# Dropping semaphore waits between the two banks of one PSUM tile, in an attention and token-mixing kernel

## The chip, the cores and the metric

The kernel runs on one core of one Trainium2 chip. The metric is the device time of one execution in microseconds (us), as a median over several executions. The profile's span is a little shorter than the timed run, because it leaves out what stands before the first and after the last instruction. Engines are named as in the profile: PE (matrix products), PEld (its weight loads), DVE (vector), ACT (scalar), POOL (gpsimd), SP (the engine that issues all DMAs here). PSUM is the memory into which PE writes its products, in eight banks; copying a finished product out of it is called an evacuation. A semaphore wait holds an engine until another engine's instruction is marked as done.

## The reference

Eight batches of 576 positions, eight heads of 64. A sliding-window attention with a distance bias is followed by a layer that mixes tokens:

```python
def _attn_ref(q, k, v):
    scores = scale * np.matmul(q, k.transpose(0, 1, 3, 2))
    mask = (rel >= 0) & (rel < window)                 # window = 128
    scores = np.where(mask, scores + bias[None], -1000000000.0)
    ...                                                # softmax
    return np.matmul(attn, v)

def _moe_ref(x, w_q, w_k, w_out):
    wq = x @ w_q
    wk = x @ w_k
    W_tok = scale * np.einsum('bsd,btd->bst', wq, wk)
    mixed = np.einsum('bst,btd->bsd', W_tok, x)
    return np.maximum(mixed, 0.0) @ w_out
```

The kernel writes the second layer as G = wk^T x, then relu(wq G), then the product with `w_out`.

## The kernel before

The work is a fixed list of 765 steps. Each step has an engine and, where it writes or reads PSUM, a bank; `PLAN` holds all of that as text, so no scheduler decides anything. Eight banks are held as four tiles of two banks each, because several steps (scores and their exponentials, transposes of q and k, MX and its relu) use two banks as one tensor. Other steps (products with `w_k` and `w_q`, G, the transposes of x, the output blocks) use one bank of a pair.

```python
pairs = [pp.tile([P, 1024], FP32, name=f"bank{i}") for i in range(4)]

def bank(b):
    return pairs[b // 2][:, 512 * (b % 2) : 512 * (b % 2) + 512]
...
def f_out(eng, bk, b=b, t=t):          # one output block: PE fills one bank
    for db in range(4):
        nc.tensor.matmul(bank(bk[0]), rm[:, b % 2, db, P * t : P * t + P],
                         wout_sb[:, db, :], start=(db == 0), stop=(db == 3))

def f_oute(eng, bk, t=t, n=n):         # ACT or DVE empties it
    copy(eng, osb[n % 3][:, t % 2, :], bank(bk[0]))
...
if t % 2:
    def f_store(eng, bk, b=b, t=t, n=n):   # two blocks leave in one DMA
        nc.sync.dma_start(out=out[b, P * (t - 1) : P * (t + 1), :].rearrange(...), in_=osb[n % 3])
...
def f_storet(eng, bk, pr=pr):          # the 64 remaining rows of two batches, in one DMA
    nc.sync.dma_start(out=out[2 * pr : 2 * pr + 2, 512:576, :], in_=osbt[pr % 2])
```

The language draws semaphore waits by itself, from who writes and reads each tile. Within one pair tile it also draws them between steps that touch different banks. A function of the kernel already takes away waits that others imply, but only those among a step's real inputs:

```python
def drop_implied(tc, order):
    ...
        if o.eng in ("ACT", "DVE", "POOL"):
            for d in implied:
                for i in o.insts:
                    for j in d.insts:
                        tc.declare_no_dep(i, j, reason="implied by another wait")
```

After the last attention step, the order on PE is: transposes and products of batches 6 and 7, with output blocks of batches 5, 6 and 7 between them. The last of them alternate over the two banks of pair 0 (`754P0`, `752P1`, `755D0`, `753D1`, `757P0`, `759P1`, `758A0`, `760A1`: PE fills bank 0, PE fills bank 1, DVE empties 0, DVE empties 1, PE fills 0 and 1, ACT empties them).

The softmax here doesn't subtract the row's maximum and nothing guards it: scores larger than these inputs give would overflow.

Of the kernel before, what the change touches and what calls it, by code (L numbers as in the profile page):

```python
# [49 lines left out]
def link(ops, rings):  # L50


    by_name = {o.name: o for o in ops}
    writers, readers, users = {}, {}, {}
    for o in ops:
        for r in o.writes:
            writers.setdefault(r, []).append(o)
        for r in o.reads:
            readers.setdefault(r, []).append(o)
    for o in ops:  # L60
        for r in o.reads:
            for w in writers[r]:
                o.deps[w.name] = w
        for ring, i in o.writes:
            old = (ring, i - rings.get(ring, FOREVER))
            for w in writers.get(old, []) + readers.get(old, []):
                o.deps[w.name] = w
                o.room.add(w.name)
        o.memory = dict(o.deps)
        for a in o.after:  # L70
            o.deps[a] = by_name[a]
        if o.opens:
            o.psum = o.opens[0]
        if o.psum:
            users.setdefault(o.psum, []).append(o)
    for us in users.values():
        opener = [o for o in us if o.opens][0]
        for o in us:
            if o is not opener:
                opener.deps.update({n: d for n, d in o.deps.items() if n in o.room})  # L80
                o.deps[opener.name] = o.memory[opener.name] = opener


def planned(ops):


    where, order = {}, []
    for item in PLAN.split():
        n, e, b = re.fullmatch(r"(\d+)([PADGS])(\d?)", item).groups()
        o = ops[int(n)]  # L90
        o.eng = {"P": "PE", "A": "ACT", "D": "DVE", "G": "POOL", "S": "SP"}[e]
        assert o.eng in o.engs and all(d.place is not None for d in o.deps.values())
        if o.opens:
            where[o.psum] = tuple(range(int(b), int(b) + o.opens[1]))
        o.banks = where.get(o.psum)
        o.place = len(order)
        order.append(o)
    assert len(order) == len(ops)
    return order
# [77 lines left out]
def drop_implied(tc, order):  # L177





    last = {}

    def covers(seen, d):
        return d.name in seen["dma"] if d.dma else seen.get(d.eng, 0) >= d.index

    def merge(a, b):
        return {e: a.get(e, frozenset()) | b.get(e, frozenset()) if e == "dma"
                else max(a.get(e, 0), b.get(e, 0)) for e in {**a, **b}}  # L190

    def ended(d):
        if d.dma:
            return merge(d.seen, {"dma": frozenset([d.name])})
        return merge(d.seen, {d.eng: d.index})

    def waited(d):
        if len(d.insts) == 1:
            return ended(d)
        if d.dma:  # L200
            return {"dma": frozenset()}
        return ended(d.before) if d.before else {"dma": frozenset()}

    for o in order:
        o.before = last.get(o.eng)
        o.index = o.before.index + 1 if o.before else 1
        seen = o.before.seen if o.before else {"dma": frozenset()}
        kept, implied = [], []
        for d in sorted(o.memory.values(), key=lambda d: -d.place):
            if covers(seen, d) or any(covers(waited(d2), d) for d2 in kept):  # L210
                implied.append(d)
            else:
                kept.append(d)
        for d in kept:
            seen = merge(seen, waited(d))
        o.seen = seen
        last[o.eng] = o
        if o.eng in ("ACT", "DVE", "POOL"):
            for d in implied:
                for i in o.insts:  # L220
                    for j in d.insts:
                        tc.declare_no_dep(i, j, reason="implied by another wait")


def steps(nc, pool, pp, q, k, v, moe_w_q, moe_w_k, moe_w_out, out):
# [407 lines left out]
@with_exitstack  # L633
def kernel(
    ctx: ExitStack,
    tc: tile.TileContext,
    q: bass.AP,
    k: bass.AP,
    v: bass.AP,
    moe_w_q: bass.AP,  # L640
    moe_w_k: bass.AP,
    moe_w_out: bass.AP,
    out: bass.AP,
):
    ctx.enter_context(tc.manual_schedule())
    pool = ctx.enter_context(tc.tile_pool(name="all", bufs=1))
    pp = ctx.enter_context(tc.tile_pool(name="psum", bufs=1, space=bass.MemoryType.PSUM))
    core = Core(tc.nc)
    ops = steps(core, pool, pp, q, k, v, moe_w_q, moe_w_k, moe_w_out, out)
    link(ops, RINGS)  # L650
    order = planned(ops)
    bias = None
    for o in order:
        o.fn(o.eng, o.banks)
        o.insts.extend(core.insts)
        core.insts.clear()
        if o.name.startswith("M") and o.eng == "DVE" and o.name[1] != "X":
            bias = o
        if o.name.startswith("cast") and o.eng == "POOL" and bias:

            tc.add_manual_dep(o.insts[0], bias.insts[0].name, mybir.DependencyInfo(
                mybir.DependencyClass.Sync, mybir.DependencyReason.DATA), reason="port")
    drop_implied(tc, order)


# [28 lines left out]
```

## Time and profile before

| | before |
|---|---|
| timed, median | 173.36 us (172.94 to 173.37, 3 runs) |
| span of the profile | 172.2 us |
| same step "WK6" (the product of batch 6 with `w_k`) begins | 137.8 us |
| last evacuation of PSUM ends | 167.6 us |
| last store lands | 171.3 us |
| semaphore-only instructions on ACT, on DVE in the trace | 52, 58 |

From the page of before: the span, and the busy time of each engine with its share of the span and its count of instructions; below it the shares of the chain of work that ended last.

```profile
span 172.2 us, 5145 instructions
...
PE 136.6 (79%) x2180; PEld 90.2 (52%) x2180; DVE 121.4 (70%) x200; ACT 124.2 (72%) x178; POOL 61.9 (36%) x82
...
PE 45%; DVE 23%; ACT 22%; issue 6%; POOL 1%; DVEq 0%; ACTq 0%; POOLq 0%
```

No engine is full over the whole span, and the average hides two stages. Here is the view by stretches of before: start and end, length, busy time of PE, PEld, DVE, ACT and POOL (with how many instructions), then the clock granted to PE, the mean share of the 16 DMA engines, and GB/s.

```profile
50.60:137.80 87.20, 80.37 (x1369) 51.93 (x1365) 75.99 (x126) 73.84 (x105) 37.39 (x47) 1.00 0.86 245
137.80:167.60 29.80, 20.63 (x174) 10.13 (x173) 9.59 (x19) 10.03 (x24) 0.00 (x0) 0.94 0.29 103
167.60:172.20 4.60, 0.00 (x0) 0.00 (x0) 0.00 (x0) 0.01 (x1) 0.00 (x0) 0.83 0.35 137
```

In the first stretch PE is busy 92% of the time. In the second, the tail, PE is busy 69%, DVE and ACT a third: nobody is full, so somebody waits for somebody. The waits view of before tells for whom (us in total, number of times, longest):

```profile
ACT osb L164 <- PE bank L164: 16.5, 6, 5.6
...
DVE osb L164 <- PE bank L164: 8.8, 4, 5.4
...
PE bank L164 <- ACT osb L164: 4.0, 8, 0.7
...
PE bank L164 <- DVE osb L164: 2.9, 4, 1.4
...
ACT osb L164 <- DVE xT L164: 1.3, 3, 0.6
```

That ACT waits for PE and PE waits for ACT is natural. The last line is not: why would an output evacuation on ACT wait for DVE to copy a transpose of x? The two share no data, only a pair tile. The timeline of the last eleven microseconds of before shows the pattern (start, length, engine, operation, output<-inputs, shape, count, and in brackets the idle time before it and what ended it):

```profile
156.68 1.02 PE L164 MATMUL bank<-wout_sb,rm 128*128 128x512 f16 x4 [0.60 <-DVE osb L164]
...
157.54 1.03 PE L164 MATMUL bank<-wout_sb,rmt 128*128 128x512 f16 x4
...
158.61 0.58 ACT L164 COPY osb<-bank 128x512 f32<-128x512 f32 x1 [1.77 <-PE bank L164]
159.24 1.02 PE L164 MATMUL bank<-wout_sb,rm 128*128 128x512 f16 x4 [0.67 <-ACT osb L164]
...
160.30 0.58 ACT L164 COPY osbt<-bank 128x512 f32<-128x512 f32 x1 [1.11 <-PE bank L164]
...
160.94 1.02 PE L164 MATMUL bank<-wout_sb,rm 128*128 128x512 f16 x4 [0.67 <-ACT osbt L164]
...
162.00 1.29 DVE L164 COPY osb<-bank 128x512 f32<-128x512 f32 x2 [5.37 <-PE bank L164]
...
163.34 3.15 PE L164 MATMUL bank<-wout_sb,rm 128*128 128x512 f16 x8 [1.38 <-DVE osb L164]
...
166.53 1.07 ACT L164 COPY osb<-bank 128x512 f32<-128x512 f32 x2 [5.64 <-PE bank L164]
```

The block that began at 156.68 is complete before 157.7 (1.02 us later). Its evacuation, the copy at 158.61, starts only when the *next* block, in the other bank of the pair, is complete too (157.54 + 1.03). Only after that copy does PE start its next block, at 159.24. The two engines take turns although there are two banks. One more thing: the eight matmuls at 163.34 take 3.15 us; eight like them took 1.90 us at 156.68 (two lines together). PE runs at half its clock there.

### The profile page before, as it was taken

The numbers are of one execution on the slowest core, as the hardware profiler recorded it, in microseconds if no ns is written. First come the engines' busy times: TensorE is split into PE (matmuls) and PEld (weight loads), VectorE is DVE, ScalarE is ACT, GpSimd is POOL, SyncE is SP. The second block draws the span as 40 slices with busy tenths as digits, with TensorE's granted clock in tenths as the row PEclk, the third lists the DMA queues.
The fourth block names the chain that finished last, engine by engine and source line by source line (L and its number), as shares of the span: only waits on it lengthen the run. The fifth ranks groups of instructions, "written<-read, shape, count | busy, mean of one in ns | idle before, by whom it ended". The sixth has DMA issues, their size and how long they took to land.

```text
span 172.2 us, 5145 instructions
## 1 busy us (share of the span) xinstructions
PE 136.6 (79%) x2180; PEld 90.2 (52%) x2180; DVE 121.4 (70%) x200; ACT 124.2 (72%) x178; POOL 61.9 (36%) x82
## 2 busy tenths in 40 slices
PE   6456597759879999999899989889699996667560
PEld 6353486557566664575664655566555662422110
DVE  4446857879799798998897878885999863331200
ACT  6999947856988889898899778997799325325120
POOL 4662245464546565457334351536221000000000
PEclk9999999987999999999999999999999999999968
DMA  5999899999973999999989999963781630403343
GB/s 174 368 224 320 236 333 249 308 358 250 224 300 91 343 316 242 266 316 356 351 236 281 305 312 235 289 122 105 207 276 62 236 125 21 156 10 122 133 150 143
DMA packets 52703, 39.39 MB, mean 229 GB/s; under 512 B 39368, under 2 KB 39368, under 8 KB 52680
## 3 DMA queue, kind: packets, MB, share of 16 engines
q1 hardware_dynamic: 52680, 39.07, 79.4%
q8 instruction: 17, 0.28, 0.7%
q14 instruction: 6, 0.05, 0.1%
HBM read 29.62 MB, written 9.44 MB: 227 GB/s over the span
## 4 chain that ended last, share of the span: by engine, by line
PE 45%; DVE 23%; ACT 22%; issue 6%; POOL 1%; DVEq 0%; ACTq 0%; POOLq 0%
PE bank L164 45%; ACT pt L164 8%; ACT table L164 5%; DVE pt L164 4%; DVE xT L164 4%; ACT osb L164 4%; DVE x L164 4%; DVE osb L164 3%; DVE qT L164 2%; DVE gm L164 2%; ACT qT L164 1%; ACT kT L164 1%; DVE wkn L164 1%; DVE wqT L164 1%; ACT osbt L164 1%
## 5 line engine op out<-in xcount | busy, mean ns | idle before, releaser
L164 ACT ACTIVATE pt<-bank 128x1024 f16<-128x1024 f32 x64 | 63.4, 1037 | 9.6 <-PE bank L164 9.6
L164 POOL CAST nat<-ld 128x1152 f16<-128x1152 f32 x32 | 36.2, 1144 | 28.0 <-DVE pt L164 16.1
L164 DVE TENSOR_TENSOR pt<-pt,table 128x2048 f16<-128x2048 f16 x32 | 38.9, 1224 | 0.7 <-ACT pt L164 0.7
L164 PE MATMUL bank<-wout_sb,rm 128*128 128x512 f16 x128 | 33.6, 391 | 6.0 <-DVE osb L164 2.0
L164 POOL CAST vt<-ldv 128x512 f16<-128x512 f32 (+1 forms) x37 | 22.0, 613 | 34.5 <-DVE pt L164 17.7
L164 PE MATMUL bank<-qT,kT 64*128 64x256 f16 (+2 forms) x320 | 26.3, 272 | 5.2 <-DVE qT L164 2.6
L164 ACT COPY osb<-bank 128x512 f32<-128x512 f32 x22 | 12.5, 590 | 19.7 <-PE bank L164 16.5
L164 PE MATMUL bank<-vt,pt 128*128 128x65 f16 x576 | 24.7, 202 | 2.0 <-DVE pt L164 1.0
L164 DVE TENSOR_TENSOR x<-bank,inv 128x640 f16<-128x640 f32 x32 | 25.7, 816 | 0.7
L164 PEld LDWEIGHTS <-pt 128*128 128x128 f16 x576 | 22.3, 103 | 6.3 <-DVE pt L164 2.1
L164 PEld LDWEIGHTS <-kT 64*128 64x128 f16 x320 | 14.6, 100 | 14.1 <-issue 10.9
L164 PEld LDWEIGHTS <-rm 128*128 128x128 f16 x128 | 11.5, 99 | 19.3 <-issue 10.0
L164 PE MATMUL bank<-ident,nat 64*128 64x64 f16 x576 | 14.9, 200 | 7.3 <-POOL nat L164 3.0
L164 PEld LDWEIGHTS <-nat 64*128 64x128 f16 x576 | 12.8, 101 | 10.9 <-POOL nat L164 5.9
L164 DVE COPY xT<-bank 128x576 f16<-128x576 f16 x32 | 13.5, 453 | 4.6 <-PE bank L164 3.6
L164 ACT ACTIVATE rm<-bank 128x512 f16<-128x512 f32 x23 | 13.9, 607 | 3.8 <-PE bank L164 3.1
L164 PE MATMUL bank<-ident,x 128*128 128x128 f16 x160 | 12.3, 222 | 2.0 <-ACT osbt L164 0.6
L164 DVE COPY osb<-bank 128x512 f32<-128x512 f32 x10 | 6.8, 687 | 9.9 <-PE bank L164 8.8
L164 ACT COPY kT<-bank 128x1152 f16<-128x1152 f16 x11 | 12.3, 1134 | 1.7 <-PE bank L164 1.7
L164 PEld LDWEIGHTS <-x 128*128 128x128 f16 x160 | 9.9, 99 | 4.9 <-issue 3.3
L164 DVE COPY qT<-bank 128x1152 f16<-128x1152 f16 x7 | 9.5, 1355 | 4.0 <-PE bank L164 3.9
L164 ACT COPY qT<-bank 128x1152 f16<-128x1152 f16 x9 | 10.1, 1124 | 1.4 <-PE bank L164 1.4
(42 smaller groups left out, 123.6 us busy)
## 6 DMA issues: line engine op xcount, KB each, us to landing
ld<-in_k_dram SPq DMA_DIRECT2D x16, 576.0 KB, 6.6
ld<-in_q_dram SPq DMA_DIRECT2D x16, 576.0 KB, 6.3
ldv<-in_v_dram SPq DMA_DIRECT2D x32, 256.0 KB, 7.5
out_dram<-osb SPq DMA_DIRECT2D x16, 512.0 KB, 5.1
ldv<-in_v_dram SPq DMA_DIRECT2D x8, 128.0 KB, 6.1
osb<-in_moe_w_out_dram SPq DMA_DIRECT2D x2, 512.0 KB, 6.8
out_dram<-osbt SPq DMA_DIRECT2D x4, 256.0 KB
osbt<-in_moe_w_k_dram SPq DMA_DIRECT2D x1, 128.0 KB, 6.3
```

The source lines that it names most:

```text
L164: r = call(*a, **k)
```

## The change

The intent: keep the order of all work, but stop drawing waits between steps that use different banks of one pair tile, unless the earlier step used a bank that the later one takes over.

```diff
+def by_banks(tc, order):
+    last, users, recent = {}, {}, {}
+    for o in order:
+        if not o.psum:
+            continue
+        before = {last[b] for b in o.banks if b in last} if o.opens else set()
+        pair = recent.setdefault(o.banks[0] // 2, [])
+        for w in pair[-48:]:
+            if w.eng == o.eng or w.psum in before or w.psum == o.psum or w.name in o.memory:
+                continue
+            for i in o.insts:
+                for j in w.insts:
+                    tc.declare_no_dep(i, j, reason="another bank, or implied")
+        for p in before:
+            o.memory.update({w.name: w for w in users[p]})
+        pair.append(o)
+        users.setdefault(o.psum, []).append(o)
+        if o.opens:
+            last.update({b: o.psum for b in o.banks})
@@
+    by_banks(tc, order)
     drop_implied(tc, order)
```

A comparison of the two built programs shows the same instructions in the same order on all five engines. Only waits differ: 194 to 154 on ACT, 209 to 170 on DVE and 267 to 276 on PE (these had been implied by waits that are gone).

## The prediction

> **What bounds the kernel now.** Span 172.2 us; the page shows PE busy 79%, ACT 72%, DVE 70%. Busy time by stretch: 60 to 142 us is PE-limited (PE 75.6 of 82 us, clock 1.00); 142 to 168 us is a tail in which nobody is full (PE 16.7 of 26 us, ACT 8.9, DVE 6.6). The timeline shows a hand-over there: matmuls fill one bank, an evacuation of 0.58 to 0.69 us runs, then PE fills the next bank of the pair. Eleven PE pauses of 0.55 to 1.38 us, together 8.0 us, lie there. The last eight output matmuls run 0.43 us apart instead of 0.215 (clock 0.6 in that slice).
>
> **What the change does.** The order on all five engines stays identical. Waits in the built program fall from 194 to 154 on ACT and 209 to 170 on DVE, and rise from 267 to 276 on PE (formerly implied). Gone are waits between users of the two banks of one pair. In the trace before, some arrived last:
> - ACT evacuations in the tail wait for PE to finish the *next* block in the partner bank: starts at 145.8, 153.7, 158.6, 160.3, 166.5 us could be 0.9 to 1.8 us earlier each.
> - DVE the same (144.2, 147.3, 150.3, 151.9, 162.0 us): 1.1 to 1.7 us each.
> - PE waits for the later of two evacuations instead of its own bank's: 12 places, 6.0 us in all, half of it between 80 and 138 us, half in the tail.
>
> Before 58 us no removed wait decided a start. The removal should be safe: the Trainium skill, "PSUM — Partial Sum Buffer", section on bank collisions, says that engines on different banks run clean; no run shows it.
>
> **On the critical path.** Laying the traced durations end to end under the new waits (an estimate from this trace's numbers alone) gives 0.4 us gained by 70 us, 0.9 by 90, 2.4 by 115, 4.4 by 140, then 9 us in the tail: last evacuation at 154.0 us instead of 167.6. By hand the same: 3 to 4.5 us in the middle, most of the tail's 8.0 us of pauses. A further 0 to 1.5 us may come from the last eight matmuls at full clock: "TensorE: Matmul & The Clock Gate", Part 1, says that the clock halves after a window of little PE activity; the 0.43 us spacing agrees. Contention and the final store are left out, so I take back 1 to 2 us.
>
> **Predicted: 160.5 us (7.4% faster), 80% range 157.0 to 165.0.** Chances: faster by over 2% 0.95, within 2% 0.04, slower 0.01.
>
> **What would show it.**
> - Tail: from 142 us to the last evacuation 25.6 us shrinks to 15 to 18; "ACT osb <- PE bank" (16.5 us) and "DVE osb <- PE bank" (8.8 us) in the waits fall by more than half.
> - First 58 us: unchanged within 0.3 us.
> - Middle: the same instruction comes 3 to 5 us earlier at 140 us; PE's busy share rises to about 85%.
> - Busy times stay within 1%, except PE, lower if the last matmuls run at full clock.
>
> **What would make it wrong.** The middle is held by PE work or by loads (a few land just before use at 121 to 129 us), so early evacuations buy nothing; the tail runs into the last batch's real chain (wkn, G, gm, MX, relu, output) or stores; denser PE work lowers the granted clock.

## The result, and the profile after

| | before | after |
|---|---|---|
| timed, median | 173.34 us (172.94 to 173.37, 4 runs) | 161.21 us (160.22 to 161.84, 4 runs) |
| ratio | | 0.930 (95% interval 0.9245 to 0.9354) |
| span of the profile | 172.2 us | 159.1 us |
| step WK1 on PE (batch 1) is under way at | 50.6 us | 48.6 us |
| step WK6 begins | 137.8 us | 132.1 us |
| last evacuation ends | 167.6 us | 150.9 us |
| last store lands | 171.3 us | 158.2 us |
| PE pauses from WK6 on (over 0.15 us, added up) | 8.0 us in 11 | none |
| semaphore-only instructions on ACT, DVE | 52, 58 | 18, 10 |

Ratios here and below are the mean time of one kernel's fast runs over that of the other's fast runs of the same rounds, so they are not quite the ratio of the medians quoted. All outputs are right.

From the page of after, the lines that answer to those of before:

```profile
span 159.1 us, 5064 instructions
...
PE 132.0 (83%) x2180; PEld 87.5 (55%) x2180; DVE 121.6 (76%) x200; ACT 123.5 (78%) x178; POOL 62.7 (39%) x82
...
PE 44%; ACT 23%; DVE 13%; DMA 5%; POOL 5%; issue 4%; POOLq 0%
```

The same work is done in 13.1 us less in these two traces. (The traced run of before took 173.91 us and that of after 160.81 us; the medians, 0.6 us lower and 0.4 us higher, differ by 12.1 us.) DMA is new in the chain: its 5% are the last store. The view by stretches of after, cut at the same instructions as before:

```profile
48.60:132.10 83.50, 79.87 (x1374) 51.18 (x1370) 76.32 (x126) 73.19 (x104) 38.01 (x47) 1.00 0.90 261
132.10:150.90 18.80, 18.14 (x178) 9.27 (x174) 9.69 (x19) 10.23 (x25) 0.00 (x0) 1.00 0.38 131
150.90:159.10 8.20, 0.00 (x0) 0.00 (x0) 0.00 (x0) 0.00 (x0) 0.00 (x0) 0.73 0.44 152
```

These three lines against those of before give the account of the span: 2.0 us are gained up to WK1, 3.7 us in the middle (87.2 to 83.5), 11.0 us in the tail (29.8 to 18.8), and 3.6 us are lost again after the last evacuation (4.6 to 8.2). Together 13.1 us. Not all of it is the change: the start-up and the slow last matmuls of before differ from run to run (see the section on the prediction). In the tail PE is now busy 96% of the time.

The waits of after: the evacuations wait less, and the line of an ACT copy that waits for DVE is gone.

```profile
ACT osb L164 <- PE bank L164: 7.1, 6, 2.7
DVE osb L164 <- PE bank L164: 4.9, 6, 2.3
...
PE bank L164 <- ACT osb L164: 1.3, 1, 1.3
```

The timeline of after, for the same blocks:

```profile
144.80 1.04 PE L164 MATMUL bank<-wout_sb,rm 128*128 128x512 f16 x4
...
145.67 1.04 PE L164 MATMUL bank<-wout_sb,rmt 128*128 128x512 f16 x4
145.87 0.58 ACT L164 COPY osb<-bank 128x512 f32<-128x512 f32 x1 [0.26 <-PE bank L164]
...
146.54 3.70 PE L164 MATMUL bank<-wout_sb,rm 128*128 128x512 f16 x16
146.75 0.58 ACT L164 COPY osbt<-bank 128x512 f32<-128x512 f32 x1 [0.29 <-PE bank L164]
...
147.61 0.69 DVE L164 COPY osb<-bank 128x512 f32<-128x512 f32 x1 [2.26 <-PE bank L164]
...
148.47 0.69 DVE L164 COPY osb<-bank 128x512 f32<-128x512 f32 x1 [0.17 <-PE bank L164]
...
150.28 0.58 ACT L164 COPY osb<-bank 128x512 f32<-128x512 f32 x1 [0.28 <-PE bank L164]
```

The copy at 145.87 starts as soon as its own block (144.80 + 1.04) is complete, while PE fills the other bank. Sixteen matmuls then run in one piece, with no bracket, so without a pause. The chain of after (start, length, what) has the whole tail as one piece of PE work:

```profile
125.14 25.12 PE bank L164 x263
150.25 0.02 issue
150.28 0.58 ACT osb L164
```

### The profile page after: what moved, and what is told of

It reads as the page before. It is cut to its first block, busy times and chain, and to the rows that moved or that the text cites. A ratio compares the mean times of both kernels' runs of the same rounds, so it can differ in the third digit from the quotient of the medians.

```text
span 159.1 us, 5064 instructions
## 1 busy us (share of the span) xinstructions
PE 132.0 (83%) x2180; PEld 87.5 (55%) x2180; DVE 121.6 (76%) x200; ACT 123.5 (78%) x178; POOL 62.7 (39%) x82
## 4 chain that ended last, share of the span: by engine, by line
PE 44%; ACT 23%; DVE 13%; DMA 5%; POOL 5%; issue 4%; POOLq 0%
PE bank L164 44%; ACT pt L164 11%; ACT table L164 6%; DMA out_dram<-osb 5%; DVE pt L164 4%; DVE x L164 3%; POOL nat L164 3%; DVE qT L164 2%; ACT qT L164 2%; ACT kT L164 2%; ACT osb L164 1%; DVE xT L164 1%; DVE inv L164 1%; DVE wkn L164 1%; DVE wqT L164 1%
## 5 line engine op out<-in xcount | busy, mean ns | idle before, releaser
L164 DVE TENSOR_TENSOR pt<-pt,table 128x2048 f16<-128x2048 f16 x32 | 39.6, 1245 | 0.3 <-ACT pt L164 0.2
L164 POOL CAST vt<-ldv 128x512 f16<-128x512 f32 (+1 forms) x37 | 22.5, 627 | 33.4 <-DVE pt L164 16.2
L164 PE MATMUL bank<-wout_sb,rm 128*128 128x512 f16 x128 | 31.7, 380 | 1.3 <-ACT osb L164 1.3
L164 PE MATMUL bank<-qT,kT 64*128 64x256 f16 (+2 forms) x320 | 25.7, 269 | 5.2 <-DVE qT L164 2.5
L164 PE MATMUL bank<-vt,pt 128*128 128x65 f16 x576 | 24.0, 199 | 1.2 <-ACT kT L164 0.7
L164 PEld LDWEIGHTS <-pt 128*128 128x128 f16 x576 | 21.8, 101 | 5.5 <-issue 1.9
L164 ACT COPY osb<-bank 128x512 f32<-128x512 f32 x22 | 13.0, 613 | 8.7 <-PE bank L164 7.1
L164 PEld LDWEIGHTS <-rm 128*128 128x128 f16 x128 | 11.0, 98 | 13.2 <-issue 2.4
L164 PEld LDWEIGHTS <-nat 64*128 64x128 f16 x576 | 12.0, 99 | 11.3 <-POOL nat L164 7.3
L164 PEld LDWEIGHTS <-x 128*128 128x128 f16 x160 | 9.3, 97 | 2.7 <-issue 1.6
```

Of the source, the lines that this page charges most:

```text
L164: r = call(*a, **k)
```

## The experiments

The theory: a wait costs time where it is the last to arrive, and nowhere else; so a third of the gain is made in the PE-limited middle, two thirds in the tail, where the false waits forced PE and the evacuating engines to take turns. Rivals: that it is the number of wait instructions that costs (79 fewer on ACT and DVE); that the gain is made in the long middle; that only PE's own waits matter. Two further questions came from the result: why the first 50 us got 2 us shorter though no false wait had decided a start there, and where the 3.6 us behind the last evacuation went.

The first six experiments use the changed kernel and limit `by_banks` by a condition on the waiting step. This is the whole edit, with the condition in place of `COND`:

```diff
-        for w in pair[-48:]:
+        for w in pair[-48:] if COND else ():
@@
-        for p in before:
+        for p in before if COND else ():
             o.memory.update({w.name: w for w in users[p]})
```

All results in one table first. Times are from the timed runs, the rest from each run's profile. "Clock" is the start of the first long record of PE at full clock (10.2 us in every trace); after it every trace has PE at half clock once more, for 3.4 or 6.8 us between 34.8 and 41.9 us. "WK1" is when that step is under way, some 0.35 us after its first matmul. Each job timed before again beside its experiments, and the ratios use those runs: their medians are 172.71 us (e1 to e4), 173.73 us (e5 to e8) and 173.36 us (e9 and e10), each job on another chip.

| run | timed, median (us) | ratio to before, 95% | clock (us) | WK1 (us) | WK1 to WK6 | WK6 to last evacuation | PE pauses from WK6 on |
|---|---|---|---|---|---|---|---|
| before | 173.34 | 1 | 27.3 | 50.6 | 87.3 | 29.8 | 8.0 in 11 |
| after | 161.21 | 0.930 (0.9245 to 0.9354) | 24.9 | 48.6 | 83.4 | 18.8 | 0 |
| e1_idle | 172.64 | 0.9995 (0.9969 to 1.002) | 25.5 | 49.0 | 87.1 | 28.4 | 8.0 in 11 |
| e2_decided | 161.96 | 0.937 (0.9338 to 0.9403) | 26.3 | 50.1 | 82.5 | 18.8 | 0 |
| e3_tail | 165.86 | 0.960 (0.9573 to 0.9632) | 24.5 | 50.1 | 87.2 | 18.8 | 0 |
| e4_early | 169.4 (fast: 168.03, 167.58) | 0.971 (0.9683 to 0.9738) | 25.0 | 48.7 | 83.3 | 28.5 | 8.0 in 11 |
| e5_evac | 164.2 | 0.945 (0.9378 to 0.9519) | 27.1 | 49.8 | 84.9 | 21.1 | 1.9 in 5 |
| e6_pe | 170.46 | 0.984 (0.9795 to 0.988) | 26.7 | 50.4 | 85.7 | 26.3 | 5.7 in 10 |

### e1: drop only the waits that decided nothing

`COND` is `o.name not in DECIDED`, where `DECIDED` names the 45 steps whose start, in the trace of before, a wait that the change removes had decided (the removed wait ended last and within 0.12 us of the start).

> The cross-bank waits are dropped for every step except the 45 whose start a dropped wait had decided in the trace of before. The program then has 42 fewer waits on ACT and 35 fewer on DVE, almost as few as the changed kernel. Theory (a wait costs only where it is the last to arrive): nothing gained, 173.3 us, at most 1% either way. Rival (every wait costs time by being carried out, so fewer waits are faster): nearly the whole gain, 161 to 163 us.

Measured: ratio 0.9995, interval 0.9969 to 1.002. The program has nearly as few waits as the changed kernel (ACT 152, DVE 174), and the trace only 16 and 18 semaphore-only instructions on ACT and DVE instead of 52 and 58. It is worth nothing, to within 0.3%. The waits view has the evacuations as in before:

```profile
ACT osb L164 <- PE bank L164: 15.1, 6, 4.9
...
DVE osb L164 <- PE bank L164: 9.9, 5, 5.4
```

Its tail keeps the 8.0 us of pauses and lasts 28.4 us, with PE at full clock throughout:

```profile
136.10:164.50 28.40, 19.33 (x174) 9.87 (x173) 9.49 (x19) 9.95 (x24) 0.00 (x0) 1.00 0.29 103
```

The rival that counts waits has fallen. The Trainium skill ("Perfetto Trace Analysis", Identifying Dependency Chains) says that an instruction that waits on several engines may have extra semaphore instructions put in front of it; traces hold such instructions, and with 76 fewer of them, on steps whose start no removed wait had decided, the time changed by no more than about 0.3%.

### e2: drop only the waits that decided

`COND` is `o.name in DECIDED`.

> The reverse: the cross-bank waits are dropped for those 45 steps alone; the program keeps about as many waits as before (ACT 199 against 194, DVE 206 against 209, PE 276 against 267). Theory: the whole gain or nearly, 160.5 to 163 us. Rival (number of waits): no gain, 173 us.

Measured: ratio 0.937, 161.96 us; the changed kernel has 0.930. The program has as many waits as before (ACT 199, DVE 206), and the trace has 58 and 51 semaphore-only instructions, yet the tail is 18.8 us long, exactly as in after, with PE busy 18.18 of it:

```profile
132.60:151.40 18.80, 18.18 (x180) 9.31 (x176) 9.70 (x19) 10.28 (x25) 0.00 (x0) 1.00 0.38 130
```

So 45 steps of 765, read off the trace of before, carry the change.

### e3 and e4: drop them in the tail only, or before it only

`COND` is `o.place >= 692` and `o.place < 692`; step 692 is WK6.

> The waits are dropped only for steps from the last 8% of the order on (those that begin after 137.8 us in before). Theory: two thirds of the gain lie there; last evacuation at about 157 to 158 us instead of 167.6, of which up to 3.5 us are lost again to the stores that follow it, so 164 to 167 us. Rival (the gain is made in the PE-limited middle): 170 us or more.

> The waits are dropped only for the steps before those. Theory: one third of the gain, last evacuation about 4 us earlier, the stores behind it unchanged, 168 to 170 us; the tail itself as long as in before (25 us from the same step on). Rival (gain in the middle): under 166 us.

Measured: 0.960 for the tail, 0.971 for what stands before it. The parts can be read off separately: with the tail alone, WK1 to WK6 takes 87.2 us as in before and the tail 18.8 us as in after; with the rest alone it is 83.3 us as in after, and the tail 28.5 us with all 11 pauses of PE. In the critical chain of e3 the tail is one piece of PE work, as in after:

```profile
135.83 19.61 PE bank L164 x196
```

Two of the four runs of e4 (171.11 and 170.77 us) count as slow because they lie over 1.5% above the fastest; only the two fast ones are in the ratio, which therefore stands on little (over all four it would be 0.980). The profile is a fast one. The "25 us" for the tail in the text before the run counts from 142 us; from WK6 the tail of before has 29.8 us. In all of e3 to e6 the last evacuation came 1 to 3 us earlier than written (156.0, 160.5, 155.9 and 162.3 us).

The tail's own gain is larger than that of the rest (11.0 us against 3.9; 9.7 us if e4's tail is the measure, in which PE kept its clock), but the timed gains (4.0% and 2.9% of some 173 us, so 6.9 and 5.0 us) are closer than that, since a part of the tail's gain is lost behind the last evacuation: from there to the last landing it is 7.4 us in e3, 5.0 us in e4. That is tested in e7 and e8.

### e5 and e6: drop them for ACT and DVE only, or for PE only

`COND` is `o.eng != "PE"` and `o.eng == "PE"`.

> The waits are dropped only where ACT or DVE waits (an evacuation that waited for the partner bank). PE keeps waiting for the later of the two evacuations. Theory: the traced durations laid end to end give a last evacuation at 157.0 us (10.6 us earlier than before), so 163 to 166 us with the stores; the greater share of the change. Rival (what counts is that PE waits for its own bank alone): 169 us or more.

> The waits are dropped only where PE waits. Theory: last evacuation 3.5 us earlier, 169 to 170.5 us; with the previous run more than 100% or less than 100% of the change shows whether the two sides help each other (laid end to end 10.6 and 3.5 add up to 14.1 against 13.6 together, so they should just about add). Rival: under 166 us.

Measured: 0.945 and 0.984. The two gains, 5.5% and 1.6%, add up to 7.1%, against 7.0% for both at once. The evacuating engines' waits for the partner bank are the greater part; PE's waits for the later of two evacuations are a small part of their own.

### e7 and e8: the stores behind the last evacuation

In after the last evacuation ends at 150.9 us and the last store lands at 158.2, 7.4 us later; in before these were 3.7 us. (In e1 and e4, which keep the waits of before in the tail but in whose traces PE did not lose its clock there, they are 5.3 and 5.0 us.) The view by stretches of after shows what the DMA engines do in that time (the two last numbers are the share of 16 DMA engines and GB/s):

```profile
151.00:154.00 3.00, 0.00 (x0) 0.00 (x0) 0.00 (x0) 0.00 (x0) 0.00 (x0) 1.00 0.99 339
154.50:156.00 1.50, 0.00 (x0) 0.00 (x0) 0.00 (x0) 0.00 (x0) 0.00 (x0) 0.55 0.13 52
156.00:157.50 1.50, 0.00 (x0) 0.00 (x0) 0.00 (x0) 0.00 (x0) 0.00 (x0) 0.50 0.13 49
```

First all 16 engines are busy; then for 3.5 us a share of 0.13, which is two of 16. In the trace each packet of 2 KB takes 84 ns there, and some 12 of them end in each half microsecond, which again is two engines at work without a pause. The landings of the two last stores of after say the same: 14 of the 16 semaphore updates of the first come by 153.1 us and the other two at 156.9 and 157.0; 14 of the last one's come by 154.8 us and two at 158.2. The store of the remainders (64 rows of two batches) has an outer dimension of 2. The Trainium skill, "DMA: Bandwidth & Descriptors", in "Why a DMA increments its semaphore by 16 and not by 1", says that the number of engines that one DMA runs on is the largest number up to 16 that divides both sides' slowest dimension that isn't 1. One side here has 2 there. The trace agrees: on the semaphore of this store, after one update at 148.3 us, two more come at 155.6 and 155.7, where the large stores have sixteen. These lines show its issue, in before and in after:

```profile
160.91 0.52 SPq L164 DMA_DIRECT2D out_dram<-osbt  x1
...
147.36 0.52 SPq L164 DMA_DIRECT2D out_dram<-osbt  x1
```

Issued at 147.36 us, this store lands at 155.7, 8.3 us later, and the two larger stores issued after it, which have their shares on the same two engines, land at 157.0 and 158.2. The edit gives each batch a DMA of its own, whose outer dimension is 64:

```diff
-                nc.sync.dma_start(out=out[2 * pr : 2 * pr + 2, 512:576, :], in_=osbt[pr % 2])
+                for i in range(2):
+                    nc.sync.dma_start(out=out[2 * pr + i, 512:576, :],
+                                      in_=osbt[pr % 2][64 * i : 64 * i + 64])
```

> Kernel before, except that each of the four stores of the 64-row remainders of two batches is issued as two DMAs of one batch each. Theory (that store, whose outer dimension is 2, is served by 2 of the 16 DMA engines for 64 packets of 84 ns each, 5.4 us, and the later stores queue behind it on these two): from the last evacuation to the end of the span 4.6 us falls by 0.5 to 1 us, since the last evacuation comes 6.7 us after that store's issue; 172 to 173 us. Rival (the end is bound by something else, such as the size of the last store): no change.

> The changed kernel with the same edit of the remainder stores. Theory: in the changed kernel the last evacuation comes only 3.5 us after the issue of that store, so the queue on two engines shows: from the last evacuation to the end of the span 8.2 us should fall to about 4.5 us, 157 to 158.5 us in all. Rival (denser stores are slow because they share bandwidth): no change, 161 us.

Measured: in the kernel before 171.12 us, ratio 0.990 (0.9825 to 0.9975); in the changed kernel 156.23 us, ratio to before 0.902 (0.8978 to 0.9059). From the last evacuation to the last landing it is 2.9 us in both; here are these 2.9 us in e8, with the DMA engines at a mean share of 0.69 instead of the long stretch at 0.13:

```profile
150.60:153.50 2.90, 0.00 (x0) 0.00 (x0) 0.00 (x0) 0.04 (x1) 0.00 (x0) 1.00 0.69 266
```

In the changed kernel the edit is thus worth 161.21 to 156.23 us, some 5 us (across two jobs); I had expected 157 to 158.5. In before it gave more than expected (171.12 us for 172 to 173), and the interval is wide; the expectation took the 3.7 us of the trace of before, where e1 and e4 have 5.3 and 5.0. The last two remainder stores of e8 land 2.5 and 2.4 us after their issue. So the time behind the last evacuation went to a store that was already bad in before, and was partly hidden there: its issue came 6.7 us before the last evacuation (160.9 and 167.6 us), in e1 and e4 5.4 us, in after only 3.5 us (147.4 and 150.9).

### e9 and e10: the very last store in two parts

The experiments pointed to a version that beats both kernels: the changed one with the spread stores. e9 adds one thing to it: the last store, of two output blocks, is issued as two DMAs of one block each. e10 is the kernel of e8 again, on the same chip.

```diff
+                    if b == NB - 1 and t == 3:
+                        for i in range(2):
+                            nc.sync.dma_start(out=out[b, P * (2 + i) : P * (3 + i), :],
+                                              in_=osb[n % 3][:, i, :])
+                        return
```

> The changed kernel with the spread remainder stores of the previous run, and in addition the very last store (two output tiles, 512 KB) issued as two DMAs of one tile, so that the first tile leaves when its own evacuation has ended, 0.87 us before the second. Theory (from the last evacuation to the end only that store is left): 0.2 to 0.8 us under the kernel with the spread stores alone, 155.5 to 156.2 us; from the last evacuation to the last landing 2.9 us falls to 2.3 to 2.6 us. Rival (the 2.9 us are latency of one store, whatever its size): no change.

> The same kernel as in the run with the spread stores in the changed kernel, again, as the partner of the previous run on the same chip: 156 to 156.7 us.

Measured: e9 155.78 us (ratio to before 0.898, 0.896 to 0.8996, one run of six slow), e10 156.17 us (0.900, 0.8981 to 0.9022). In the profiles the time from the last evacuation to the last landing falls from 2.9 to 2.5 us, as expected, but in the timed runs the 0.3 us between the means of the fast runs (155.72 and 156.01 us) lie inside the scatter of either. Inconclusive in time; shown in the profile.

## Why the prediction was right, and where it was off

The prediction was 160.5 us in a range of 157 to 165; measured are 161.21 us. Point by point:

- **The mechanism held.** e2 shows that the 45 steps found in the trace of before carry the gain (0.937 of 0.930), e1 that the rest carries none. The tail, e3 and e4, and the two sides, e5 and e6, came out within the ranges written before the runs, but for one of the two fast runs of e4, which lies a little under (167.58 us for 168 to 170).
- **The middle: right in size, missed as stated.** 4.4 us were predicted by 140 us, and "3 to 5 us earlier" for the same instruction; WK6 comes 5.8 us earlier, of which 1.9 us are the start-up below. Cut at WK1, the gain up to WK6 is 3.9 us in after (87.3 to 83.4), 4.8 in e2 and 4.0 in e4. The pauses of PE over 0.15 us in that stretch fall from 6.1 us in 16 to 2.8 us in 7.
- **The tail: right, at the edge.** Some 9 us were predicted, and up to 1.5 us more if the last eight matmuls kept the full clock; measured are 11.0 us from WK6 on. Counted from the copy to `osbt` at 141.78 us (135.62 in after), 25.8 us became 15.2, where 15 to 18 was written. The 8.0 us of PE pauses are gone to the last one. Some 1.3 us are the last matmuls at full clock, and those are not owed to the change alone: in e1, e4 and e7, which keep the pauses, the tail is 28.4 to 28.5 us long, with no record of half clock before the last evacuation, while the traced run of before had 29.8. Without them the waits are worth 9.6 to 9.7 us in the tail. "TensorE: Matmul & The Clock Gate", Part 1, says that the clock halves after an idle window, and that the window runs freely. In the trace of before the clock fell at 163.8 us, in the traces without pauses not before the last evacuation. The stretch before that fall was not idle, though: PE was busy 1.5 of the 3.4 us. That e1, e4 and e7 kept the clock with the same pauses would fit a window that runs freely; no run tests it.
- **The end: under-sized, the step that failed.** The prediction said "Contention and the final store are left out, so I take back 1 to 2 us". Between the two main traces the final stores took back 3.7 us (7.4 instead of 3.7 from the last evacuation to the last landing). Some of that is the traced run of before, whose slow last matmuls gave the store more time: against e1 and e4 (5.3 and 5.0 us) it is 2.1 to 2.4 us, a little over the 1 to 2 us that the prediction allowed. The name "final store" was right; the cause, a store on two DMA engines, was not seen. It could have been: in before the same store is issued at 160.9 us and lands at 168.8.
- **The first 58 us: wrong as stated.** "Unchanged within 0.3 us" was measured as 2.0 us earlier at WK1. No part of it is shown to be the change. The traces fall into two groups. Six have an early record of full clock, at 4.3 to 5.3 us, then one of half clock (after, e1, e4, e7, e8, e10); in these WK1 is under way at 48.6 to 49.4 us. The other six have none (before, e2, e3, e5, e6, e9); in these it is at 49.8 to 50.6. Kernels with and without the waits are in both groups: e7, whose waits are those of before, has 49.3, and e8, with the whole change, 49.4. It stays open what puts a run in one group or the other.
- **Luck.** The last evacuation came 3 us earlier than predicted (150.9 for 154.0), and the start-up (2.0 us) and the clock of the last matmuls (1.3 us) make up that much; the stores gave most of it back. That these offset each other, so that the total is closer than its terms, is luck. Against e1, a trace of the same start-up group with the full clock in its tail, the change gives 0.4 us up to WK1 (less than the scatter inside the group), 3.6 in the middle and 9.6 in the tail, and loses 2.1 at the end: about 11.5 us of span, where the traced durations laid end to end had 13.6 less 1 to 2.
- **Smaller marks.** The evacuations' waits for PE fell by 57% on ACT (16.5 to 7.1) and 44% on DVE (8.8 to 4.9), where more than half was predicted for both. PE's share rose to 83% for 85%. PE's busy time fell by 3.4%, more than the last eight matmuls explain; it is a modelled time in a trace, and POOL's rose by 1.3% where 1% was allowed.
- **Safety.** "PSUM — Partial Sum Buffer", PSUM bank collisions raise a hardware error, says that engines on different banks run clean. All kernels without these waits ran to the end with the right result; none of these runs tests what would happen in one bank.

## What to carry to other kernels

A tile that spans two banks is one object to whatever draws the waits; if its banks are used one by one, look in the trace for an engine that waits for another with which it shares no data. Count a wait only where it ended last: reading those 45 steps from one trace, and laying the traced durations end to end without them, gave the middle and the tail to within 2 us, while the number of waits told nothing. When a change makes the end of a kernel denser, look at what used to be hidden behind its slack: here a store with an outer dimension of 2 took back 2 to 4 us, and three lines of source bring 161.2 down to 156.2 us.

## What the Trainium skill lacked or had wrong

- "TensorE: Matmul & The Clock Gate", Part 1, says that the moment of warming up varies by about half a microsecond, and that the ramp is under 1% of a kernel and not to be fitted. Here the first long record of full clock starts at 24.5 to 27.3 us, after a stretch in which PE is far from full (12.1 of the first 22 us in after), and the kernel before has two groups of times in one and the same job (e5 to e8): 172.46 and 172.59 us with a mean granted clock of 0.933, 173.36 to 173.85 us with 0.974 to 0.976. That is 0.7%: inside the page's 1%, but too much where a per cent is measured. That the start-up clock makes the two groups is not shown. The mean clock does not tell them apart either: in that job the faster runs have the lower one, but in the job of e9 runs at 0.920 to 0.924 took 173.34 to 173.37 us, and the fastest run of e2 has 0.978. It is misleading, since the trace of before holds no clock record before 27.3 us, while others have an early record of half clock (in after from 7.9 to 24.9 us).
- No page was found with the price of a wait that is already satisfied: 77 fewer waits in the program on ACT and DVE (e1) changed the time by 0.05%, with an interval of 0.3% below to 0.2% above.
- "PSUM — Partial Sum Buffer" tells to guard PSUM by bank and quadrant, or more simply by bank, but not that waits drawn by tile couple the banks of a tile that spans two; here that cost 12.1 us of 173.3.
- "DMA: Bandwidth & Descriptors" has the rule by which an outer dimension of 2 confines a DMA to two engines, and this case agrees (a share of 0.13 of 16 engines for 3.5 us). It does not draw the consequence that later stores over all 16 engines end late behind such a store: two of 512 KB issued 1.8 and 3.5 us after it landed 1.3 and 2.6 us after it.
